# Diagonal blocks of the last 64 queries as full-row products, and an instruction order that counts array-form changes

## The chip, the cores and the metric

The kernel runs on one core of a Trainium2 chip. The metric is the device time of one launch in microseconds. Three runs of the kernel before took 1037.78, 1039.32 and 1043.57 us; their median, 1039.32 us, is the time before. One further execution was profiled.

A core has a matrix engine (TensorE, in the profile PE, with its weight loads shown apart as PEld), a vector engine (VectorE, DVE), a scalar engine (ScalarE, ACT), a general engine (GpSimd, POOL) and a sequencer that issues the DMAs (SyncE, SP). They run their own instruction queues side by side and wait for one another through semaphores.

## The reference

Attention with a decay and a causal mask, then a feed-forward block. The shapes are 8 batches, 8 heads, 576 positions, head size 64, and 4608 tokens by 512, with 2048 hidden columns.

```
scores = q @ k.T / sqrt(64) + cum[:, None] - cum[None, :]    # cum: running sum of log f
scores = where(causal, -1e9, scores);  attn = softmax(scores);  x = attn @ v
h = x @ w_in;  g = h * tanh(log1p(exp(min(h, 20))))          # for h <= 20;  out = g @ w_out
```

576 queries are four blocks of 128 and a last block of 64. This last block of 64 queries, with its own 64 keys, is the "diagonal block" of the title.

## The kernel before

Heads are taken in pairs: one group `g` is two heads (`j` = 0, 1) of one batch, 32 groups in all. Matrices are kept as pairs of 16-bit halves, high and low, so that one exact product is three 16-bit products. Groups 0 to 6 go the old way (`max_items`, `st_items`, `pv_items`): scores are computed transposed (keys in the partitions), the row maxima are found beforehand and put in as an extra row, and P times V takes the exponentials as 32-bit weights. Groups 7 to 31 go the new way (`new_st_items`, `new_pv_items`): scores have queries in the partitions, DVE adds the mask and finds the maxima in one instruction (`highest`), ACT exponentiates, ACT and DVE split the result into halves (`turn`), and a transposing DMA turns it. Behind each batch's attention come the feed-forward products, spread between the later groups' attention.

The last 64 queries of both heads share the 128 partitions: head 0 in 0 to 63, head 1 in 64 to 127. PE works on them with weights of 64 columns, two products side by side in the two halves of the array (`beside`, line 1050). For the diagonal block the weights also have 64 rows only, because keys of head 0 and of head 1 lie in different partitions. Thus PE uses three forms of its array, which the profile writes as rows*columns: 128*128, 128*64 (70 rows count as 128) and 64*64. The places with 64*64 are:

- `tail` (line 1347), new way: the 64 queries of both heads against four key blocks from tile `W` (24 products of form 128*64, in pairs), and then against the diagonal block from tile `V` (6 products of form 64*64, in pairs). `V` is made in `w_` (line 1301): `pv` holds the diagonal scores of both heads in 64 columns, ACT writes their exponentials into `ev`, and these 64 columns are read twice (`two`, line 1318) to fill the 128 columns of `hv`, which a DMA turns into `tv`.
- `blocks` of `pv_items` (line 1399), old way: for `kt == 4` one 32-bit product of 64 rows from tile `T4`, once for each of two heads.
- `two_pass` (line 1161) in `k4`, old way: for groups below 6 the causal mask is added by a product `msk` times `idm` cut to 64 by 64, between products of form 128*64.

The order of instructions on each engine is not the order of the code. `Program` records all operations and runs a list scheduler over them (`forward`, line 410; `backward`, line 370): each engine has a heap of ready operations by rank, and a table of costs says how long each would take. The recorded operations are emitted from one line, so nearly all instructions of the profile carry L317. In that table a PE operation costs its columns divided by the clock; a narrow product beside another one costs 22 ns, and a pair of `beside` adds 53 columns for its second product (line 199). A change of the array's form costs nothing in it. `warmed` (line 319) fills PE's idle time at the start with products of an identity (`idm,idh`).

Of the kernel before, what the change touches and what calls it, by code (L numbers as in the profile page):

```python
# [131 lines left out]
PRIO = 200  # L132
WARM0 = 8000.0
# [21 lines left out]
class Program:  # L155
# [9 lines left out]
    def __init__(self, nc):  # L165
        self.nc = nc
        self.ops = []
        self.banks = []
        self.sets = []
        self.rank = None  # L170
# [10 lines left out]
    def choose(self, *ways):  # L181

        r, w, opts = [], [], []
        for way in ways:
            total, port = 0.0, False
            for eng, method, a, kw in way:
                aps = [(k, x) for k, x in list(enumerate(a)) + list(kw.items()) if hasattr(x, "tensor")]
                w += [z for k, x in aps if k in ("out", "accum_out", 0) for z in self.region(x)]
                r += [z for k, x in aps if k not in ("out", "accum_out", 0) for z in self.region(x)]
                if eng == "scalar":  # L190
                    (r if method == "activation" else w).append(("table", 0, 1, 0, 1))
                if eng == "tensor":

                    w.append((w[0][0] + "/pe", 0, 1, 0, 1))
                port |= self.shared(eng, method, aps)
                cost = self.cost(eng, method, kw, aps)
                if isinstance(cost, tuple) and total:

                    total = (total[0] + 53, total[1] + cost[1], 0)
                else:  # L200
                    total = cost if isinstance(cost, tuple) else total + cost + (80 if total else 0)
            opts.append((eng, way, total, port))
# [8 lines left out]
        self.leads.append(self.lead)  # L211
        func = ways[0][0][3].get("func") if ways[0][0][0] == "scalar" and len(ways) == 1 else None
        self.sets.append("mish" if func == AF.Mish else "exp" if func == AF.Exp else None)
        if self.sets[-1] and self.phase is not None:
# [6 lines left out]
            if hasattr(x, "tensor") and x.space == PSUM})  # L221

# [187 lines left out]
    def forward(self, deps, succ, rank):  # L410
# [13 lines left out]
        table = "exp"  # L424

# [27 lines left out]
        while len(order) < n:  # L453
# [20 lines left out]
            while ripe[q]:  # L474
# [53 lines left out]
            else:  # L528
                if q == "tensor":
# [6 lines left out]
                    half = h  # L536
                elif lock:
# [74 lines left out]
def attn_moe(ctx: ExitStack, tc: tile.TileContext, qk, v, f, w_in, w_out, out):  # L612
# [44 lines left out]
    nc.vector.tensor_scalar(out=mskb2, in0=msk2, scalar1=2.0**100, scalar2=None, op0=ALU.mult)  # L657
    ones = cp.tile([P, P], F32, name="ones")
# [497 lines left out]
    def st_items(g):  # L1156
# [25 lines left out]
        def finish(ps, tag, n, sel):  # L1182
            t4 = n < CH
            e = sp.tile([P, n], F32, name=f"e{tag}{g}", tag="e4" if t4 else "pt", bufs=2 if t4 else NPT)
# [28 lines left out]
        def k4():  # L1213
# [4 lines left out]
            def sel(e):  # L1218
                for j in range(2):
                    tri(e[j * D : (j + 1) * D], 1, D)  # L1220

            finish(ps, "T4", D, sel)
# [10 lines left out]
    def new_st_items(g):  # L1233
# [12 lines left out]
        def highest(o, c, m, first=3e38):  # L1246

            nc.vector.tensor_tensor_reduce(
                out=o, in0=o, in1=m, scale=-0.125, scalar=first, op0=ALU.add, op1=ALU.min,
# [51 lines left out]
        def w_():  # L1301
# [16 lines left out]
            two = ev.unsqueeze(1).to_broadcast([P, 2, D])  # L1318
            hh, ll = (h[:, i].rearrange("p (a d) -> p a d", a=2) for i in range(2))
            nc.choose(*(scaled(hh, two, None, x) for x in HW))  # L1320
            nc.choose(*(sub(ll, two, hh, x) for x in LW_))
# [8 lines left out]
    def new_pv_items(g):  # L1330
# [3 lines left out]
        def products(o, t, k, c, vh, vl, first, last, r=slice(0, P)):  # L1334
            n = 2 if s["V"] is t else 8
            hh, ll = t[r, k, c], t[r, n // 2 + k, c]
# [10 lines left out]
        def tail(o):  # L1347
            for kt in range(5):
                both = []
                for j in range(2):  # L1350
                    r = slice(j * D, (j + 1) * D)
                    if kt < 4:
                        both.append(products(
                            o[r], s["W"], kt, r, s["vh"][:, 2 * kt + j], s["vl"][:, 2 * kt + j], kt == 0, False))
                    else:
                        both.append(products(o[r], s["V"], 0, r, s["vh"][r, 8], s["vl"][r, 8], False, True, r))
                for x in zip(*both):
                    beside(*x)
# [23 lines left out]
    def pv_items(g):  # L1382
# [3 lines left out]
        def pblk(j, kt, qt):  # L1386
            if qt == 4:
                if kt == 4:
                    return "T4", slice(0, D)
# [9 lines left out]
        def blocks(o, j, qt):  # L1399
# [3 lines left out]
            for kt in kts:  # L1403
                tg, c = pblk(j, kt, qt)
                if kt == 4:
                    r = slice(j * D, (j + 1) * D)
                    mm(o[0:m], s[tg][r, c], s["vf"][r, 8], False, False)
# [503 lines left out]
```

## Time and profile before

| | |
|---|---|
| runs, median | 1039.32 us (1037.78 to 1043.57) |
| the profiled execution | 1038.15 us, of which the span of instructions is 1036.4 us |
| mean granted clock of PE | 0.995 |
| PE busy | 1000.0 us, 7779 matmuls |
| DVE busy, ACT busy | 738.9 us, 703.0 us |
| POOL busy | 12.8 us |

Matmuls are pipelined: a row shows a matmul from its start until its result is out, so the next one starts long before. What a matmul occupies of PE is the distance from its start to the next start. Rows that follow each other with the same tiles and engine are merged into one with a count; the first form stands for all of them.

### The profile page before, as it was taken

What the parts mean: (1) busy time and instruction counts of PE and PEld (TensorE: products, weight loads), DVE (VectorE), ACT (ScalarE), POOL (GpSimd) and SP (SyncE); (2) the same over time, 40 slices, a digit from 0 to 9 for tenths busy, and PEclk for the clock granted to TensorE, in tenths of its full rate; (3) what the DMA queues carried; (4) which work ended last, traced back from release to release, by engine and by line L of the source; (5) the groups of instructions that cost most, each with busy time, mean ns of one, the idle gap of its engine ahead of it and who ended that gap; (6) DMA issues with size and microseconds to landing.
All of it is one profiled execution on the core that took longest, in us unless ns stands there. A gap on an engine that the chain in (4) does not pass through costs nothing.

```text
span 1036.4 us, 20830 instructions
## 1 busy us (share of the span) xinstructions
PE 1000.0 (96%) x7779; PEld 561.9 (54%) x7779; DVE 738.9 (71%) x2043; ACT 703.0 (68%) x1309; POOL 12.8 (1%) x73
## 2 busy tenths in 40 slices
PE   5899999999999999999999999999999999999998
PEld 4787565544454455445555455454544555656664
DVE  8878978998776677777766777676766559962432
ACT  7566788978776767777777777787687675433322
POOL 1000001000000000000000000000000000000000
PEclk8999999999999999999999999999999999999999
DMA  7868736599866767677767766767566423001001
GB/s 219 263 185 230 241 105 172 131 216 240 174 138 149 166 138 148 139 177 145 156 136 164 150 153 140 166 141 142 116 123 135 85 56 93 2 3 41 1 1 42
DMA packets 245410, 140.45 MB, mean 136 GB/s; under 512 B 213436, under 2 KB 214012, under 8 KB 245308
## 3 DMA queue, kind: packets, MB, share of 16 engines
q1 hardware_dynamic: 245308, 139.12, 57.8%
q8 instruction: 61, 1.00, 0.4%
q14 instruction: 41, 0.34, 0.1%
HBM read 47.78 MB, written 11.76 MB: 57 GB/s over the span
## 4 chain that ended last, share of the span: by engine, by line
PE 61%; DVE 15%; ACT 10%; DMA 8%; issue 4%; SPq 2%; POOL 0%; DVEq 0%; ACTq 0%; POOLq 0%
PE b L317 61%; DMA pt<-hb 2%; DMA st<-hl 2%; DMA qk<-in_qk_dram 2%; DVE b L317 2%; DVE wall L317 2%; ACT junk L317 2%; SPq L317 2%; ACT hb L317 2%; ACT st L317 1%; DVE hl L317 1%; DVE hb L317 1%; ACT more_e L317 1%; DVE vv L317 1%; DVE x L317 1%
## 5 line engine op out<-in xcount | busy, mean ns | idle before, releaser
L317 PEld LDWEIGHTS <-wall 128*128 128x128 f16 x3372 | 321.6, 98 | 354.4 <-issue 21.2
L317 PE MATMUL b<-gh,wall 128*128 128x512 f16 x1152 | 369.3, 379 | 1.2 <-DVE wall L317 0.7
L317 PE MATMUL b<-xa,wall 128*128 128x512 f16 (+1 forms) x1602 | 344.2, 365 | 6.1 <-ACT me L317 4.1
L317 PE MATMUL b<-gl,wall 128*128 128x512 f16 x576 | 218.2, 379 | 0.0
L317 PE MATMUL b<-st 70*128 70x256 f16 (+10 forms) x978 | 145.6, 280 | 16.9 <-DMA st<-cumd 7.3
L317 DVE SCALAR_TENSOR_TENSOR gl<-me,gsc,gh 128x512 f16<-128x512 f32 x144 | 106.5, 750 | 36.1 <-ACT gh L317 34.6
L317 PEld LDWEIGHTS <-st 128*128 128x128 f16 (+3 forms) x1170 | 91.2, 101 | 72.0 <-issue 26.0
L317 ACT ACTIVATE me<-b,cinv 128x512 f32<-128x512 f32 (+1 forms) x130 | 85.3, 661 | 59.3 <-PE b L317 58.5
L317 PE MATMUL b<-vv,pt 128*128 128x64 f16 (+3 forms) x2492 | 116.4, 207 | 2.8 <-ACT pt L317 1.3
L317 ACT ACT_TABLE_LOAD x74 | 94.9, 1283 | 1.5 <-DVE cinv L317 0.2
L317 DVE CUSTOM_DVE_ANT_0 b<-b,mskw 128x512 f32<-128x512 f32 (+2 forms) x150 | 84.9, 567 | 12.8 <-PE b L317 10.7
L317 ACT ACTIVATE more_e<-b,mn 128x512 f32<-128x512 f32 (+3 forms) x114 | 59.1, 540 | 34.0 <-DVE mn L317 31.8
L317 ACT ACTIVATE st<-b,mn 128x512 f32<-128x512 f32 (+3 forms) x111 | 57.5, 547 | 29.3 <-DVE mn L317 26.6
L317 PEld LDWEIGHTS <-pt 128*128 128x128 f16 (+1 forms) x2100 | 65.0, 101 | 17.4 <-DMA pt<-hb 2.1
L317 DVE TENSOR_TENSOR hb<-st,hb 128x512 f16<-128x512 f32 x75 | 51.6, 689 | 30.9 <-ACT hb L317 28.7
L317 DVE TENSOR_TENSOR hb<-more_e,hb 128x512 f16<-128x512 f32 x75 | 51.4, 688 | 28.5 <-ACT hb L317 28.4
L317 ACT ACTIVATE gh<-me,gsc 128x512 f16<-128x512 f32 x84 | 60.1, 719 | 2.0
L317 DVE TENSOR_SCALAR gh<-me,gsc 128x512 f16<-128x512 f32 x60 | 28.9, 485 | 39.2 <-ACT me L317 38.2
L317 ACT ACTIVATE hb<-st 128x512 f16<-128x512 f32 x75 | 46.8, 627 | 10.0 <-DMA pt<-hb 8.1
L317 ACT ACTIVATE junk<-qk 128x576 bf16<-128x576 f32 x60 | 40.7, 678 | 17.9 <-DMA qk<-in_qk_dram 17.4
L317 ACT ACTIVATE hb<-more_e 128x512 f16<-128x512 f32 x75 | 46.7, 626 | 6.6 <-DMA pt<-hb 6.1
L317 DVE SCALAR_TENSOR_TENSOR hl<-qk,qt,hl 128x576 f16<-128x576 f32 x58 | 46.0, 814 | 5.2 <-DMA st<-hl 3.7
(167 smaller groups left out, 1004.7 us busy)
## 6 DMA issues: line engine op xcount, KB each, us to landing
st<-hl SPq DMA_DIRECT2D x180, 144.0 KB
qk<-in_qk_dram SPq DMA_DIRECT2D x30, 576.0 KB
v<-in_v_dram SPq DMA_DIRECT2D x32, 288.0 KB
out_dram<-ot SPq DMA_DIRECT2D x36, 256.0 KB
wall<-in_w_in_dram SPq DMA_DIRECT2D x16, 512.0 KB
wall<-in_w_out_dram SPq DMA_DIRECT2D x16, 512.0 KB
pt<-hb SPq DMA_TRANSPOSE x150
part<-ot SPq DMA_DIRECT2D x8, 256.0 KB
```

The costliest lines, as they stand in the source:

```text
L317: r = getattr(real[eng], method)(*a, **kw)
```

## The change

Four edits on the diagonal blocks, one on the scheduler.

1. `tail`: the tile `V` becomes block-diagonal over 128 columns, so its three products take all 128 rows and 128 columns and serve both heads at once. They stand at the head of the accumulation, not at its end.
2. `w_`: `highest` for `pv` reads the 64 columns twice, adds a mask of 128 columns that shuts out the other head (`mskv`), and writes 128 columns beside the scores in the same bank; the exponential then covers 128 columns and goes to a fixed tile `evs`, one of two by the group's number.
3. `k4` and `blocks`, old way: the exponentials of both heads go to two diagonal places of `evs`, which is zero elsewhere, with one ACT instruction for each head. The product of `T4` takes 128 rows, with form 128*64.
4. `two_pass`: the mask product takes all 128 rows of `msk` and `idm`, which for 64 columns is form 128*64.
5. `Program`: each PE operation records its form. In `forward` a change of form costs 97 ns at full clock; while PE is in a narrow form, it takes ready operations of the same form first, up to 3000 units of rank ahead of others. The second product of a pair adds 8 columns in place of 53.

```
-                    total = (total[0] + 53, total[1] + cost[1], 0)
+                    total = (total[0] + 8, total[1] + cost[1], 0)
...
+        self.forms.append(self.form(*ways[0][0]) if ways[0][0][0] == "tensor" else None)
...
+    def form(eng, method, a, kw):
+        rows = int(kw["in_"].shape[0] if method == "transpose" else kw["lhsT"].shape[0])
+        cols = int(kw["out"].shape[0])
+        return rows > 64 or (rows + 31) // 32, cols > 64 or (cols + 31) // 32
...
-                if q == "scalar" and f not in (None, table):
+                if q == "scalar" and f not in (None, table) or q == "tensor" and self.forms[x[1]] != form:
...
-                if far is not None and x[0] > far[0] + TSWAP:
+                if far is not None and x[0] > far[0] + (TSWAP if q == "scalar" else 0 if form == (True, True) else MSWAP):
...
+                    if self.forms[i] != form:
+                        form = self.forms[i]
+                        cost += MSW * slow
...
+    evs = cp.tile([P, 2, P], F32, name="evs")
+    nc.gpsimd.memset(evs, 0.0)
+    mskv = cp.tile([P, 2, D], BF16, name="mskv")
+    nc.gpsimd.memset(mskv, -60000.0 * 2.0**100)
+    for j in range(2):
+        r = slice(j * D, (j + 1) * D)
+        nc.gpsimd.tensor_copy(out=mskv[r, j], in_=mskb2[r])
...
-                mm(o[:, 0:tri], msk[0:tri, 0:tri], idm[0:tri, 0:tri], False, False)
+                mm(o[:, 0:tri], msk[:, 0:tri], idm[:, 0:tri], False, False)
...
+            s["T4"] = evs[:, g % 2].rearrange("p (j d) -> p j d", j=2)
+            for j in range(2):
+                r = slice(j * D, (j + 1) * D)
+                e = s["T4"][r, j]
+                nc.scalar.activation(out=e, in_=ps[r, 0:D], func=AF.Exp, scale=0.125)
...
-            highest(pv[:, 0:D], 9, mskb2)
+            two = pv[:, P : 2 * P].rearrange("p (j n) -> p j n", j=2)
+            highest(two, 9, mskv, 3e38, pv[:, 0:D].unsqueeze(1).to_broadcast([P, 2, D]))
...
-            ev = sp.tile([P, D], F32, name=f"ev{g}", tag="e4")
-            exp(ev, pv[:, 0:D], 8)
+            ev = evs[:, g % 2]
+            exp(ev, pv[:, P : 2 * P], 8)
...
         def tail(o):
...
+            for a in products(o, s["V"], 0, slice(0, P), s["vh"][:, 8], s["vl"][:, 8], True, False):
+                mm(*a)
+            for kt in range(4):
+                for x in zip(*(products(
+                        o[r], s["W"], kt, r, s["vh"][:, 2 * kt + j], s["vl"][:, 2 * kt + j], False, kt == 3)
+                        for j, r in enumerate((slice(0, D), slice(D, P))))):
                     beside(*x)
...
-                    r = slice(j * D, (j + 1) * D)
-                    mm(o[0:m], s[tg][r, c], s["vf"][r, 8], False, False)
+                    mm(o[0:m], s[tg][:, j], s["vf"][:, 8], False, False)
```

How the order moves on PE, at the first tail of a new group. Before, the pairs from `W` (tile `pt`) end, six narrow products from `V` (tile `tv`) follow, and then a feed-forward product (`gh`, `wall`). The size at a row's end is that of the output.

```order
L317 LDWEIGHTS pt_138
L317 MATMUL b_0_128<-vv_142,pt_138 64x65
L317 LDWEIGHTS pt_138
L317 MATMUL b_0_128<-vv_142,pt_138 64x65
L317 LDWEIGHTS tv_196
L317 MATMUL b_0_128<-vv_142,tv_196 64x65
L317 LDWEIGHTS tv_196
L317 MATMUL b_0_128<-vv_142,tv_196 64x65
L317 LDWEIGHTS tv_196
L317 MATMUL b_0_128<-vv_142,tv_196 64x64
```

After the change, at the same tail, a full product of the block before (`pt_141`), the three from `V`, and then the first pair from `W`:

```order
L327 LDWEIGHTS pt_141
L327 MATMUL b_0_130<-vv_143,pt_141 128x65
L327 LDWEIGHTS tv_196
L327 MATMUL b_0_130<-vv_143,tv_196 128x65
L327 LDWEIGHTS tv_196
L327 MATMUL b_0_130<-vv_143,tv_196 128x64
L327 LDWEIGHTS tv_196
L327 MATMUL b_0_130<-vv_143,tv_196 128x65
L327 LDWEIGHTS pt_139
L327 MATMUL b_0_130<-vv_143,pt_139 64x65
L327 LDWEIGHTS pt_139
L327 MATMUL b_0_130<-vv_143,pt_139 64x65
```

The products from `V` are three of 128 outputs in place of six of 64, and they stand among full products.

The second place on PE is the end of a later tail (tile `pt_142`). After the change the scores of the last 64 queries of another group (`st`) stand directly behind it, before the feed-forward product that follows:

```order
L327 LDWEIGHTS pt_142
L327 MATMUL b_0_130<-vv_132,pt_142 64x65
L327 LDWEIGHTS st_1_85
L327 MATMUL b_0_123<-st_1_85 64x64
L327 LDWEIGHTS st_1_85
L327 MATMUL b_0_123<-st_1_85 64x64
L327 LDWEIGHTS st_1_88
L327 MATMUL b_0_123<-st_1_88 64x64
```

Before the change the six products from `V` end every such run of narrow products, as in the first fence, and the scores of the last 64 queries stand in runs of their own. Now 14 of the 25 tails have such scores in the same run.

The third place is ACT near the start, at the first exponential of a diagonal block of the old way. Before:

```order
L317 ACTIVATE pt_134<-b_0_119 128x512
L317 ACTIVATE junk_110,wsq<-wall 128x512
L317 ACTIVATE e_0_132<-b_0_122 128x64
L317 ACTIVATE pt_137<-b_0_123 128x512
L317 ACTIVATE pt_138<-b_0_128 128x512
```

After:

```order
L327 ACTIVATE mr_131<-b_0_123 128x128
L327 ACTIVATE junk_112,wsq<-wall 128x512
L327 ACTIVATE evs<-b_0_124 64x64 x2
L327 ACTIVATE pt_134<-b_0_129 128x512
L327 ACTIVATE pt_135<-b_0_121 128x512
```

One instruction of 128 partitions has become two of 64, and it stands before the wide exponentials of this group and not between them.

Over the whole program PE's order holds 249 changes of the array's form before and 169 after, and 141 and 135 filling products.

## Rows read from the trace of the kernel before

**Rows 1.** The page: span, and busy time, share and instructions by engine.
```profile
span 1036.4 us, 20830 instructions
...
PE 1000.0 (96%) x7779; PEld 561.9 (54%) x7779; DVE 738.9 (71%) x2043; ACT 703.0 (68%) x1309; POOL 12.8 (1%) x73
```

**Rows 2.** Stages: length, busy us of PE, PEld, DVE, ACT, POOL; clock, DMA.
```profile
0.00:40.00 40.00, 24.97 (x268) 20.73 (x268) 35.02 (x90) 26.31 (x56) 3.88 (x32) 0.87 0.81 258
40.00:140.00 100.00, 96.12 (x879) 70.81 (x879) 79.99 (x236) 68.33 (x142) 0.81 (x6) 1.00 0.67 198
140.00:300.00 160.00, 156.41 (x1113) 83.77 (x1112) 135.22 (x402) 134.04 (x242) 5.37 (x15) 1.00 0.76 180
300.00:860.00 560.00, 550.57 (x4390) 279.92 (x4389) 389.64 (x1106) 408.82 (x755) 2.77 (x20) 1.00 0.66 138
860.00:1036.40 176.40, 171.96 (x1137) 106.65 (x1135) 99.08 (x214) 65.47 (x116) 0.00 (x0) 1.00 0.08 24
```

**Rows 3.** Waits of PE: for whom, us in total, times, longest.
```profile
PE b L317 <- ACT me L317: 4.1, 7, 1.1
PE b L317 <- ACT st L317: 2.6, 7, 0.8
```

**Rows 4.** Timeline of PE around narrow scores: start, us, instruction, count.
```profile
250.94 0.59 PE L317 MATMUL b<-gh,wall 128*128 128x512 f16 x2
251.37 0.38 PE L317 MATMUL b<-gl,wall 128*128 128x512 f16 x1
251.59 0.38 PE L317 MATMUL b<-gh,wall 128*128 128x512 f16 x1
251.90 0.69 PE L317 MATMUL b<-st 70*64 70x64 f16 x8
```

**Rows 5.** Timeline of PE around an old group's mask products.
```profile
42.10 0.22 PE L317 MATMUL b<-st 128*128 128x128 f16 x1
42.15 0.22 PE L317 MATMUL b<-msk,idm 128*128 128x128 f16 x1
42.30 0.22 PE L317 MATMUL b<-st 128*64 128x64 f16 x1
42.45 0.21 PE L317 MATMUL b<-idm,msk 64*64 64x64 f16 x1
42.59 0.22 PE L317 MATMUL b<-mr,more_e 128*64 128x64 f16 x1
```

**Rows 6.** Timeline of PE: full products from `pt`; the six of a tail's `tv`.
```profile
205.53 1.07 PE L317 MATMUL b<-vv,pt 128*128 128x65 f16 x30
206.44 0.38 PE L317 MATMUL b<-gh,wall 128*128 128x512 f16 x1
...
246.80 0.28 PE L317 MATMUL b<-vv,tv 64*64 64x65 f16 x6
247.02 0.39 PE L317 MATMUL b<-gh,wall 128*128 128x512 f16 x1
```

**Rows 7.** Groups of PE and PEld: count, busy us, mean ns, idle before.
```profile
L317 PE MATMUL b<-vv,tv 64*64 64x65 f16 x100 | 7.0, 202 | 0.0
L317 PE MATMUL b<-vv,e 64*64 64x65 f32 x28 | 4.6, 243 | 0.0
L317 PE MATMUL b<-idm,msk 64*64 64x64 f16 x12 | 2.6, 213 | 0.0
L317 PEld LDWEIGHTS <-pt 128*128 128x128 f16 (+1 forms) x2100 | 65.0, 101 | 17.4 <-DMA pt<-hb 2.1 <-issue 1.7
```

**Rows 8.** Groups of DVE and ACT: the instructions of 64 and 128 columns.
```profile
L317 DVE CUSTOM_DVE_ANT_0 b<-b,mskb 128x128 f32<-128x128 f32 x50 | 15.0, 300 | 4.8 <-PE b L317 3.4
L317 DVE CUSTOM_DVE_ANT_0 b<-b,mskb 128x64 f32<-128x64 f32 x25 | 5.8, 233 | 2.2 <-PE b L317 2.2
L317 ACT ACTIVATE st<-b,mn 128x128 f32<-128x128 f32 x24 | 8.8, 368 | 1.7 <-DVE mn L317 1.7
L317 ACT ACTIVATE e<-b,mn 128x64 f32<-128x64 f32 x25 | 7.8, 313 | 0.6 <-DVE mn L317 0.6
L317 ACT ACTIVATE e<-b 128x64 f32<-128x64 f32 x7 | 1.6, 222 | 3.3 <-PE b L317 3.1
```

More of the change, by code (lines that the diff above doesn't have):

```diff
@@ L132 @@
 PRIO = 200
+MSW = 97.0
+MSWAP = 3000
 WARM0 = 8000.0
@@ L169, in __init__ @@
         self.sets = []
+        self.forms = []
         self.rank = None
@@ L221, in choose @@
             if hasattr(x, "tensor") and x.space == PSUM})
+    @staticmethod
+    def form(eng, method, a, kw):
+        rows = int(kw["in_"].shape[0] if method == "transpose" else kw["lhsT"].shape[0])
+        cols = int(kw["out"].shape[0])
+        return rows > 64 or (rows + 31) // 32, cols > 64 or (cols + 31) // 32
     @staticmethod
@@ L424, in forward @@
         table = "exp"
+        form = (True, True)
         left, half = {}, 0
@@ L1182, in finish @@
         def finish(ps, tag, n, sel):
-            t4 = n < CH
-            e = sp.tile([P, n], F32, name=f"e{tag}{g}", tag="e4" if t4 else "pt", bufs=2 if t4 else NPT)
+            e = sp.tile([P, n], F32, name=f"e{tag}{g}", tag="pt", bufs=NPT)
             nc.scalar.activation(out=e, in_=ps[:, 0:n], func=AF.Exp, scale=0.125)
@@ L1216, in k4 @@
                 two_pass(ps[j * D : (j + 1) * D, 0:D], j, slice(CH, S), slice(CH, S), D)
[L1218 to L1222, printed above, removed]
+            s["T4"] = evs[:, g % 2].rearrange("p (j d) -> p j d", j=2)
[3 more added lines that the diff above has]
+                nc.scalar.activation(out=e, in_=ps[r, 0:D], func=AF.Exp, scale=0.125)
+                if g >= GS:
+                    tri(e, 1, D)
         return [
@@ L1244, in scores, with highest @@
             mm(o, q2[:, j, q0 : q0 + m], k2[:, j, k0 : k0 + n], False, True)
-        def highest(o, c, m, first=3e38):
+        def highest(o, c, m, first=3e38, in_=None):
             nc.vector.tensor_tensor_reduce(
-                out=o, in0=o, in1=m, scale=-0.125, scalar=first, op0=ALU.add, op1=ALU.min,
+                out=o, in0=o if in_ is None else in_, in1=m, scale=-0.125, scalar=first, op0=ALU.add, op1=ALU.min,
                 accum_out=s["mx"][:, c : c + 1])
@@ L1317, in w_ @@
             t = sp.tile([P, 2, P], F16, name=f"tv{g}", tag="tv", bufs=2)
[L1318 to L1321, printed above, removed]
+            nc.choose(*(scaled(h[:, 0], ev, None, x) for x in HW))
+            nc.choose(*(sub(h[:, 1], ev, h[:, 0], x) for x in LW_))
             nc.sync.dma_start_transpose(out=t, in_=h)
@@ L1332, in new_pv_items, with products @@
         s = st[g]
-        def products(o, t, k, c, vh, vl, first, last, r=slice(0, P)):
+        def products(o, t, k, c, vh, vl, first, last):
             n = 2 if s["V"] is t else 8
-            hh, ll = t[r, k, c], t[r, n // 2 + k, c]
+            hh, ll = t[:, k, c], t[:, n // 2 + k, c]
             return [(o, hh, vh, first, False), (o[:, 0:D], hh, vl, False, False), (o, ll, vh, False, last)]
@@ L1347, in tail @@
         def tail(o):
-            for kt in range(5):
-                both = []
-                for j in range(2):
-                    r = slice(j * D, (j + 1) * D)
[L1352 to L1357, printed above, removed]
+            for a in products(o, s["V"], 0, slice(0, P), s["vh"][:, 8], s["vl"][:, 8], True, False):
[4 more added lines that the diff above has]
+                        for j, r in enumerate((slice(0, D), slice(D, P))))):
                     beside(*x)
@@ L1388, in pblk @@
                 if kt == 4:
-                    return "T4", slice(0, D)
+                    return "T4", None
                 return f"T2{j}", slice(256 + D * kt, 320 + D * kt)
@@ L1405, in blocks @@
                 if kt == 4:
-                    r = slice(j * D, (j + 1) * D)
-                    mm(o[0:m], s[tg][r, c], s["vf"][r, 8], False, False)
+                    mm(o[0:m], s[tg][:, j], s["vf"][:, 8], False, False)
                     continue
```

## The prediction

> **What bounds the kernel now.** I read the page's busy shares first. PE is busy for 1000.0 of 1036.4 us, DVE for 738.9, ACT for 703.0 [rows 1]. The stages come next, for the share over the span hides where PE stands idle. In the first 40 us PE is idle for 15.0 us (40.00 − 24.97): that is the start, with loads and preparation ahead of the first scores. From 40 to 860 us it is idle for 3.9 + 3.6 + 9.4 = 16.9 us in 820, and behind 860 for 4.4 us [rows 2]. So from 40 us on PE sets the pace. DVE and ACT come closest from 140 to 300 us, with 135.2 and 134.0 us of 160, 84%. The waits that PE does have are short and scattered: the largest kind from the middle part is seven waits for ACT's `me` with 4.1 us together, none over 1.1 us [rows 3].
>
> A busy PE is not a PE at its peak, so the third view is the distance between starts. A 512-column product is followed by its like after 0.22 us (251.37 to 251.59). When the next product has the form 70*64, it starts 0.31 us later (251.59 to 251.90), and PE was not waiting for data, since the row shows no idle time [rows 4]. At an old group the same is seen three times in a row: 0.05 us from a 128-column product to the next of its form, 0.15 us to the first of form 128*64, 0.15 us from there into 64*64 and 0.14 us out of it [rows 5]. A 64-column product takes about half of the 0.05 us by itself (30 full products of 65 columns took 0.91 us, 0.030 each [rows 6]). So a change of form costs 0.31 − 0.22 = 0.09, 0.15 − 0.05 = 0.10, and 0.15 − 0.03 = 0.12 or 0.14 − 0.03 = 0.11 us. I take 0.095 us: the two readings that compare the same product before and after a change. The bounds are 0.09 and 0.11. This cost stands within PE's busy time and in no wait.
>
> **The change part by part.** Changes of form: PE's order holds 249 before and 169 after, 80 fewer. They come from four places. (a) Each of 25 tails went 128*128, 128*64, 64*64 and back, and now goes 128*128, 128*64 and back: 25 fewer. The count of tails is that of the `tv` products of 65 columns, 100 with four to a tail [rows 7]. (b) The 32-bit products from `T4` are 28 records, two to a product, hence 14 products in 14 accumulations [rows 7]; each dropped one change: 14. (c) Twelve mask products of 64*64 stood between narrow ones [rows 7]; a run of that kind costs two changes where 128*64 lies on both sides, as in rows 5, else one: 21 by the order. (d) The remaining 80 − 60 = 20 are ten runs of narrow products that have been joined to others. At 0.095 us this is 80 × 0.095 = **7.6 us** less on PE (7.2 to 8.8 by the bounds). Laid against the trace, 15 of the 249 lie in the first 40 us, 3 behind 860 us and all others where PE sets the pace.
>
> Products of `V`: six narrow ones with the change behind them took 0.22 us (246.80 to 247.02), so 0.125 without the change; three full ones take 3 × 0.030 = 0.09 [rows 6]. That is 0.035 × 25 = **0.9 us** less. The bounds: each new product might need its weight load in full, 101 ns [rows 7], which would make it 25 × (0.303 − 0.125) = 4.5 us more; and at best the three are free, 3.1 us less. I take the value by the 30 products, because each of those has its own weight load too and still starts 0.030 us after the last.
>
> At this place the Trainium skill speaks against the change. Its page "TensorE: Matmul & The Clock Gate", section "Back-to-back issue gap", says that in a stream of weight load and matmul pairs both set the pace, and that 128-column products come about 81 ns apart. With that, an estimate, 75 products would take 6.1 us and not 2.3, and the sum would be 3.8 us worse than mine. The trace does not agree: its 30 pairs come 30 ns apart.
>
> The products from `T4` stay two records each and keep their columns, and so do the mask products: their rows double, and rows are not what a product's duration goes by here (`vv,e` with 64 rows has 243 ns [rows 7], and I found none longer for more rows). I cost them at nothing.
>
> DVE and ACT: `highest` on the diagonal block goes from 64 to 128 columns, 300 against 233 ns, 25 × 0.067 = 1.7 us of DVE; its exponential from 313 to about 368 ns, 25 × 0.055 = 1.4 us of ACT; in the old way one exponential of 222 ns becomes two, at most 7 × 0.222 = 1.6 us of ACT [rows 8]. The halving of `ev` and the turning DMA had 128 columns already. Together 4.7 us, hidden where PE never waits for these tiles (idle before the `tv` products: 0.0 us [rows 7]), and up to 4.7 us more if every one were on the path. The products of `V` now come first in the tail. They can't be late on that account: the tail still needs all of `W`, whose turning is issued behind that of `V`. POOL gets two memsets and two small copies at the start, when it has 3.9 us of work in 40 [rows 2].
>
> What is late next: PE now asks for everything 8.5 us earlier by the end of the attention part, and the waits of 16.9 us between 40 and 860 us can grow. The order also is a new one at every engine, so no single wait of before has to stand. I add **1.0 us**; the bounds are all 8.5 us given back, and 5 us gained if the order, which now counts what PE really takes, has fewer waits (nearly a third of 16.9). I stay near zero since PE waits for DVE and ACT only one part in fifty, and they have a sixth of their time free even at the tightest stage.
>
> The sum against the profiled execution: 1038.15 − 7.6 − 0.9 + 1.0 = 1030.65 us. The median of the runs stands 1.17 us above that execution, so I forecast 1030.65 + 1.17 = **1031.8 us**, by itself between 1029 and 1034.
>
> **Rivals.** First, PE is shorter, but the waits come back: half or more of 8.5 us turns into waits for DVE and ACT. For it speaks the stage from 140 to 300 us, in which both are at 84% and the first weights, the last old groups and the new ones meet; against it, that stage holds only 37 of the 249 changes. With 5 us given back the time is 1036.
>
> Second, the order gains as well. It now knows 97 ns for a change, which is what the rows show, so an operation is released nearer to when PE is ready for it. Taking away a third of 16.9 us gives 1031.8 − 1.0 − 5 = 1026 us. Against it: most waits of before are single ones of under 1.1 us with a dozen different releasers [rows 3].
>
> Third, and on the other side: the grouping holds banks. While PE is in the narrow form, it takes narrow products ahead of others. In the new order 12 of 25 groups have the 512-column scores of the last queries apart from their diagonal scores (before: 2). The wide `highest` starts from the maximum of the diagonal scores, so a bank that is written early stays taken until the others have come. If each of these 12 and of the 14 tails that are joined with scores made PE wait 0.6 us (the mean of seven waits for `me`, 4.1 / 7 [rows 3]), it would cost 26 × 0.6 = 15.6 us and give 1030.8 + 15.6 = 1046. It decides from 0.53 us per place, where the 8.5 saved and 5.2 more are used up. Against it: where they are apart, it is mostly by one tail's length, some 30 products and under 1 us, and there are four score banks.
>
> Fourth, the change does what it says, but full products need their weight load on the path: a full product from `V` then costs 0.101 us, the 4.5 us of above in place of the 0.9 saved, which gives 1031.8 + 5.4 = 1037 us. It is the skill's rule carried to its end; the 30 products in 0.91 us speak against it.
>
> **How the numbers follow.** A measurement of this kernel can tell 0.5% from no change, 5.2 us: faster is below 1034.1, slower above 1044.5. The forecast has a chance of 0.57, all of it on the faster side; the gaining order 0.15, faster; the waits that come back 0.19, no change; the weight loads 0.03, no change; the held banks 0.06, slower. Hence faster 0.72, same 0.22, slower 0.06. The range from 1026 to 1038 us holds the forecast, nearly all of the two cases of no change, and about half of the gaining order.
>
> **What would show it.** In the profile after, PE has no 64*64 form; the `tv` products are 75 of form 128*128, three in about 0.09 us; a feed-forward product still starts 0.31 us ahead of a narrow one; PE's busy time falls by 7 to 9 us to about 992, and its idle time from 40 to 860 us stays between 12 and 22 us. I am wrong in the size if the busy time does not fall by that much, in the hiding if the idle time grows by more than 5 us, and about the start if the first 40 us become longer, which I cost at nothing since the order of PE there is nearly the same.

## The result, and the profile after

The changed kernel takes 1029.12 us (median of 4 runs, 1027.53 to 1030.69), beside 1040.03 us of the kernel before in the same comparison (4 runs): the ratio is 0.9893 [0.9871, 0.9915]. A second comparison gave 1030.03 beside 1039.8 us, 0.9914 [0.9895, 0.9934]. So 9.8 to 10.9 us went, where 7.5 were forecast (1039.32 − 1031.8). The profiled execution is the fastest of the first four, 1027.53 us.

The page's span, and its line of busy time by engine:

```profile
span 1025.7 us, 20649 instructions
...
PE 988.8 (96%) x7698; PEld 556.1 (54%) x7698; DVE 737.0 (72%) x2040; ACT 707.0 (69%) x1315; POOL 13.4 (1%) x77
```

Beside [rows 1], PE is busy for 11.2 us less, and the span is 10.7 us shorter. Span less busy time, which is PE's idle time over the whole run, is 36.9 us after and was 36.4. So nearly all that was gained stands within PE's busy time, as the change of form did, and PE waits about as much as it did. A part of such a difference is the clock: the profile grants PE either the full clock (1.00) or half of it (0.50), and PE was busy at half clock for 6.8 us in the profile before and for 4.3 us here. About half of that time, 3.4 and 2.2 us, is lost (an estimate).

The stages, with the columns of [rows 2] (length; busy us of PE, PEld, DVE, ACT, POOL; clock, DMA share, GB/s):

```profile
0.00:40.00 40.00, 24.05 (x267) 19.79 (x267) 34.69 (x91) 26.23 (x57) 4.83 (x35) 0.91 0.80 249
40.00:140.00 100.00, 94.71 (x903) 71.06 (x903) 86.29 (x256) 75.31 (x159) 0.77 (x7) 1.00 0.75 209
140.00:300.00 160.00, 156.26 (x1148) 83.57 (x1149) 129.13 (x385) 130.57 (x238) 5.14 (x16) 1.00 0.75 175
300.00:860.00 560.00, 551.90 (x4351) 280.31 (x4349) 400.40 (x1131) 412.67 (x754) 2.64 (x19) 1.00 0.67 140
860.00:1025.70 165.70, 161.85 (x1039) 101.40 (x1037) 86.46 (x182) 62.23 (x110) 0.00 (x0) 1.00 0.06 20
```

From 40 to 860 us PE is idle for 5.3 + 3.7 + 8.1 = 17.1 us; it was 16.9 [rows 2]. The first 40 us hold as many products as before (267 and 268), so the start did not become longer. What is gained shows as a shorter last stage, 165.7 us and 1039 products in place of 176.4 us and 1137: the work behind 860 us is what had not been reached by then.

PE's waits (whom for, us in total, times, longest), with the two kinds of [rows 3]:

```profile
PE b L327 <- ACT me L327: 6.7, 9, 1.7
...
PE b L327 <- ACT st L327: 3.4, 5, 1.4
...
PE b L327 <- ACT evs L327: 0.4, 1, 0.4
```

The waits for `me` and `st` rose by 2.6 and 0.8 us, the others fell by 2.3 us together; all of PE's waits went from 31.4 to 32.5 us. On `evs`, the new tile, PE waited once, for 0.4 us.

The timeline of PE: an old group's mask products (as in [rows 5]), a tail (as in [rows 6]), and narrow scores behind a feed-forward product (as in [rows 4]); start, us, instruction, count:

```profile
43.61 1.90 PE L327 MATMUL b<-vv,pt 128*128 128x65 f32 x16
45.44 0.46 PE L327 MATMUL b<-st 128*64 128x512 f16 x4
45.70 0.23 PE L327 MATMUL b<-idm,msk 128*64 128x64 f16 x2
45.73 0.23 PE L327 MATMUL b<-mr,more_e 128*64 128x64 f16 x2
45.77 0.23 PE L327 MATMUL b<-st 128*64 128x64 f16 x2
45.92 1.26 PE L327 MATMUL b<-vv,pt 128*128 128x65 f32 x10
...
241.66 1.08 PE L327 MATMUL b<-vv,pt 128*128 128x65 f16 x30
242.58 0.25 PE L327 MATMUL b<-vv,tv 128*128 128x65 f16 x3
242.76 0.57 PE L327 MATMUL b<-vv,pt 128*64 128x65 f16 x24
243.26 0.39 PE L327 MATMUL b<-gh,wall 128*128 128x512 f16 x1
...
247.84 0.38 PE L327 MATMUL b<-gh,wall 128*128 128x512 f16 x1
248.15 0.69 PE L327 MATMUL b<-st 70*64 70x64 f16 x8
```

The mask products (45.70) now start 0.03 us ahead of their neighbours of the same form, with nothing between, where [rows 5] had 0.14 to 0.15 on either side. The three products from `tv` take 0.18 us up to the first narrow product (242.58 to 242.76), and 0.097 of it is the change of form that stood there before too: 0.08 for three. And a feed-forward product still starts 0.31 us ahead of a narrow one (247.84 to 248.15): the price of a change is what it was, there are fewer.

The price can be summed over a whole trace, from the distance between starts less what the same product takes among its like (stretches at half clock and places with a wait left out). Before, 239 changes take 23.5 us, 0.098 each; after, 163 take 15.7 us, 0.096 each. That is 7.8 us less. Too short a wait leaves no idle time in these rows, since a product's row (0.38 us) is longer than the distance to the next (0.31 us). That these distances are the price and no waits for data is shown by their evenness: the 14 from a feed-forward product to a 70*64 one are all between 0.307 and 0.310 us.

One place gained more than a change. The last narrow 32-bit product from `pt`, the product of `T4` (tiles `e` and `evs`, two records) and the next full product, before and after:

```profile
68.35 0.22 PE L317 MATMUL b<-vv,pt 128*64 128x65 f32 x1
68.50 0.33 PE L317 MATMUL b<-vv,e 64*64 64x65 f32 x2
68.75 0.32 PE L317 MATMUL b<-vv,pt 128*128 128x65 f32 x1
...
68.79 0.22 PE L327 MATMUL b<-vv,pt 128*64 128x65 f32 x1
68.85 0.28 PE L327 MATMUL b<-vv,evs 128*64 128x65 f32 x2
69.06 0.32 PE L327 MATMUL b<-vv,pt 128*128 128x65 f32 x1
```

From the first row to the third it is 0.40 us before and 0.27 after; over the 14 places the medians are 0.406 and 0.267. So 0.139 us went at each, and not only the 0.095 of one change: beside the change ahead of it, the first record of the product became 0.048 us shorter. That is 0.6 us more than the prediction has.

Groups of PE, DVE and ACT that answer to [rows 7, 8] (count, busy us, mean ns, idle before):

```profile
L327 PE MATMUL b<-vv,tv 128*128 128x65 f16 x50 | 6.3, 192 | 0.0
...
L327 PE MATMUL b<-vv,tv 128*128 128x64 f16 x25 | 4.8, 193 | 0.0
L327 PE MATMUL b<-vv,evs 128*64 128x65 f32 x28 | 3.9, 222 | 0.0
...
L327 PE MATMUL b<-idm,msk 128*64 128x64 f16 x12 | 1.7, 200 | 0.0
...
L327 DVE CUSTOM_DVE_ANT_0 b<-b,mskv 128x128 f32<-128x128 f32 x25 | 7.6, 303 | 2.7 <-PE b L327 2.7
...
L327 ACT ACTIVATE evs<-b,mn 128x128 f32<-128x128 f32 x25 | 9.1, 363 | 4.3 <-DVE mn L327 4.3
...
L327 ACT ACTIVATE evs<-b 64x64 f32<-64x64 f32 x14 | 3.0, 215 | 0.5 <-PE b L327 0.2
```

No group has the form 64*64 any more. `highest` on the diagonal costs 1.8 us more (7.6 against 5.8), the exponentials 2.7 us more (9.1 + 3.0 against 7.8 + 1.6), nearly as worked out ahead (1.7 and 3.0).

### The profile page after: what moved, and what is told of

The parts are those of the page before. It is cut to its first block, busy times and chain, and to the rows that moved or that the text cites. A ratio compares the mean times of both kernels' runs of the same rounds, so it can differ in the third digit from the quotient of the medians.

```text
span 1025.7 us, 20649 instructions
## 1 busy us (share of the span) xinstructions
PE 988.8 (96%) x7698; PEld 556.1 (54%) x7698; DVE 737.0 (72%) x2040; ACT 707.0 (69%) x1315; POOL 13.4 (1%) x77
## 4 chain that ended last, share of the span: by engine, by line
PE 60%; ACT 6%; DVE 5%; DMA 4%; issue 2%; SPq 0%; ACTq 0%; DVEq 0%
PE b L327 60%; DMA pt<-hb 3%; DVE b L327 2%; ACT hb L327 1%; ACT L327 1%; DVE vv L327 1%; ACT more_e L327 1%; ACT st L327 1%; DMA st<-hl 1%; ACT me L327 1%; DVE x L327 1%; DVE xp L327 1%; DVE hb L327 1%; ACT ot L327 0%; DMA v<-in_v_dram 0%
## 5 line engine op out<-in xcount | busy, mean ns | idle before, releaser
L327 PE MATMUL b<-st 70*128 70x128 f16 (+12 forms) x978 | 144.9, 280 | 15.9 <-DMA st<-cumd 6.8
L327 DVE CUSTOM_DVE_ANT_0 b<-b,mskw 128x256 f32<-128x256 f32 (+2 forms) x150 | 84.5, 566 | 8.4 <-PE b L327 6.3
L327 ACT ACTIVATE gh<-me,gsc 128x512 f16<-128x512 f32 x89 | 63.5, 719 | 2.1
L327 DVE TENSOR_SCALAR gh<-me,gsc 128x512 f16<-128x512 f32 x55 | 26.6, 484 | 37.8 <-ACT me L327 36.8
L327 PEld LDWEIGHTS b<-vv,pt 128*128 128x128 f32 x392 | 45.2, 183 | 5.6 <-ACT pt L327 2.5
```

The lines of the kernel that those rows point to most:

```text
L327: r = getattr(real[eng], method)(*a, **kw)
```

## The experiments

All times are medians of several runs, beside runs of the kernel before on the same chip; those of one set share them (before: 1039.8 in the first, 1039.48 in the second, 1040.13 us in the third). The kernel after ran in the first set only; the three figures of before lie within 0.7 us, and a difference of 1 us between sets decides nothing. "Changes" counts the changes of form in PE's order. The last three columns are of the profiled execution: PE's busy time, the part of it in stretches with a granted clock of 0.50, and idle, which is span less busy time.

| kernel | changes | us | ratio | PE busy | at half clock | PE idle |
|---|---|---|---|---|---|---|
| before | 249 | 1039.8 | 1 | 1000.0 | 6.8 | 36.4 |
| after (repeated) | 169 | 1030.03 | 0.9914 [0.9895, 0.9934] | 991.7 | 15.8 | 35.8 |
| blocks alone | 195 | 1036.26 | 0.9972 [0.9957, 0.9986] | 997.1 | 16.0 | 36.6 |
| scheduler alone | 231 | 1034.95 | 0.9961 [0.9946, 0.9976] | 1000.7 | 16.0 | 33.8 |
| `V` in three places | 312 | 1050.98 | 1.0105 [1.0083, 1.0128] | 1010.0 | 13.1 | 39.2 |
| extra DVE and ACT work | 168 | 1030.76 | 0.991 [0.9898, 0.9923] | 991.7 | 9.8 | 37.9 |
| no grouping | 191 | 1034.13 | 0.9949 [0.993, 0.9968] | 995.5 | 13.2 | 38.8 |
| pair at 53 columns | 162 | 1033.86 | 0.995 [0.9932, 0.9968] | 990.2 | 8.6 | 41.0 |
| scores as one | 156 | 1021.88 | 0.983 [0.9814, 0.9846] | 989.9 | 11.0 | 33.2 |
| other ranks 1 | 162 | 1035.2 | 0.9961 [0.9942, 0.998] | 988.9 | 4.4 | 42.2 |
| other ranks 2 | 168 | 1031.1 | 0.992 [0.9891, 0.9949] | 994.6 | 14.6 | 38.3 |
| ranks 2, scores as one | 156 | 1027.36 | 0.9894 [0.9865, 0.9923] | 992.1 | 11.7 | 36.0 |
| no grouping, scores as one | 184 | 1034.17 | 0.9944 [0.9922, 0.9966] | 995.6 | 13.1 | 37.9 |

The columns of the profile are read together. If half of the time at half clock is taken off the busy time (an estimate), it goes with the count of changes: 1003.5 us at 312, 996.6 at 249, 992.6 at 231, 989 from 195 to 184, and 984 to 987 from 169 to 156. The idle time, from 33 to 42 us, does not go with that count.

**The changed kernel again.** The same file, to have its size with a second set of runs.

> The changed kernel again, as the yardstick of this set. Its order holds 169 changes of the array's form, that of before 249. Theory A (each change that goes saves about 0.097 us of PE, and nothing else of size happens): the first timing was 1029.1 against 1040.0, 10.9 us, of which A explains 80 x 0.097 + 0.9 = 8.7; a repeat should come out at 8 to 11 us below before. Theory B (the new order brings a good part by fewer waits): the same here, the kernels below tell the two apart.

It gave 1030.03 us (4 runs, 1029.55 to 1030.93): 9.8 us less than before.

**The block edits alone.** The blocks as after, the scheduler as before (no price, no grouping, 53 columns):

```
-                    total = (total[0] + 8, total[1] + cost[1], 0)
+                    total = (total[0] + 53, total[1] + cost[1], 0)
...
-        self.forms.append(self.form(*ways[0][0]) if ways[0][0][0] == "tensor" else None)
+        self.forms.append((True, True) if ways[0][0][0] == "tensor" else None)
```

> The four edits on the diagonal blocks alone; the scheduler prices as before (no form, 53 for the second of a pair). Its order holds 195 changes, 54 fewer than before. Theory A: 54 x 0.097 + 0.9 for the products of V = 6.1 us less than before, about 1034 where before has 1040. Theory B: less than half of the changed kernel's gain, so 1035 to 1040, as its order is not the new one.

1036.26 us, 3.5 less than before. With 54 changes fewer the count alone gives 54 × 0.097 = 5.2 and the products of `V` 0.9, hence 1034. That is missed by 2.6 us. The order holds 162 filling products, 21 more than before; at 0.055 us each they can be some 1.2 us of this, an estimate. The rest is not explained.

**The scheduler edits alone**, on the blocks of before (edit 5 of the change and nothing else):

```
-                    total = (total[0] + 53, total[1] + cost[1], 0)
+                    total = (total[0] + 8, total[1] + cost[1], 0)
...
+                    if self.forms[i] != form:
+                        form = self.forms[i]
+                        cost += MSW * slow
```

> The kernel before with the scheduler's edit alone (price of a form change, grouping, 8 for the second of a pair); the diagonal blocks stay narrow. Its order holds 231 changes, 18 fewer than before. Theory A: 18 x 0.097 = 1.7 us less than before, about 1038. Theory B: 4 to 6 us less, 1034 to 1036.

1034.95 us, 4.9 less, where 18 changes fewer are worth 1.7. In its profile PE's busy time is that of before, and its idle time is 2.6 us shorter. But this execution has one of the stretches at half clock of the last section, from 38.1 to 48.4 us, with PE busy throughout: 16.0 us of busy time at half clock, where before has 6.8. That hides some 4.6 us of shorter busy time (half of the difference, an estimate), and the idle time that is less lies in that stretch and behind it, 3.4 us from 40 to 300 us in place of 7.5. So that this order gains by its waits is not shown; 3.2 of the 4.9 us stay without a cause. Parts and whole do not add up either: 3.5 + 4.9 = 8.4 of 9.8 us.

**The three products of `V` apart.** In the tail, one of them stands behind each of the first three key blocks, so that each needs a change of form before and behind it:

```
             for kt in range(4):
...
                     beside(*x)
+                if kt < 3:
+                    mm(*vs[kt])
```

> The changed kernel with the three full products of V put one each behind the first three key blocks of the tail, so that PE goes from narrow to full and back three times in each of 25 tails. Same products, same sizes; its order holds 312 changes, 143 more than the changed kernel. Theory A: 143 x 0.097 = 13.9 us more than the changed kernel, about 1043. If the price seen between starts were covered in the end by other waits, it would stay within 5 us of the changed kernel.

1050.98 us, 21.0 more than after. The order holds 143 changes more: 143 × 0.097 = 13.9 us by the price. The timeline of PE in one tail:

```profile
247.88 0.20 PE L327 MATMUL b<-vv,tv 128*128 128x64 f16 x1
248.02 0.28 PE L327 MATMUL b<-vv,pt 128*64 128x65 f16 x6
248.23 0.20 PE L327 MATMUL b<-vv,tv 128*128 128x65 f16 x1
248.37 0.29 PE L327 MATMUL b<-vv,pt 128*64 128x65 f16 x6
248.59 0.39 PE L327 MATMUL b<-gh,wall 128*128 128x512 f16 x1
```

One full product that takes 0.03 us among its like holds PE for 0.14 us when a narrow one follows (247.88 to 248.02, and 248.23 to 248.37). A wait for data would not be so regular: behind the 50 products of 65 columns the distance is 0.133 to 0.135 us, 0.104 above the product's own, a little more than at the other kinds of change. Summed from the starts as above, 303 changes take 30.0 us here, and 161 take 15.5 us in the repeated kernel after. The page gives 18.3 us more of busy time than in the repeated kernel after, and 3.4 more idle. The changes cover 14.5 of the 18.3, and 15 more filling products (150 against 135) of 0.055 us another 0.8; the rest, some 3, I could not assign.

**Extra work on DVE and ACT.** `highest` and the exponential of the diagonal block are each issued twice, 25 times:

```
+            highest(two, 9, mskv, 3e38, pv[:, 0:D].unsqueeze(1).to_broadcast([P, 2, D]))
             highest(ps, 8, mskw[:, 0:1].to_broadcast([P, CH]), s["mx"][:, 9:10])
...
             exp(ev, pv[:, P : 2 * P], 8)
+            exp(ev, pv[:, P : 2 * P], 8)
```

> The changed kernel with the DVE instruction on the diagonal scores (0.300 us) and its exponential on ACT (0.37 us) issued twice in each of the 25 new groups, with the same result: 7.5 us more of DVE and 9.2 us more of ACT, against the 1.7 and 1.4 us that the change added there. Its order holds 168 changes. If this work is hidden, as the prediction has it: within 2 us of the changed kernel, 1029 to 1032. If it stands on the path that sets the end: 8 to 17 us more, 1038 to 1047.

1030.76 us, against 1030.03 and 1029.12 of the kernel after. The groups, with the two instructions (count, busy us, mean ns):

```profile
L327 DVE CUSTOM_DVE_ANT_0 b<-b,mskv 128x128 f32<-128x128 f32 x50 | 15.1, 302 | 2.9 <-PE b L327 2.5
...
L327 ACT ACTIVATE evs<-b,mn 128x128 f32<-128x128 f32 x50 | 18.4, 368 | 4.7 <-DVE mn L327 4.3
```

7.5 us more on DVE and 9.3 us more on ACT, one behind the other in each of 25 groups, cost about 1 us, no more than the runs scatter. The order is a new one here too, which by itself can move the time by several us (below), so this shows that most of the added work is hidden, and not what each us of it costs. The 4.5 us that the change itself adds there are a quarter of it.

**Without grouping, and with the old price of a pair.** Two single edits of the scheduler, each on the kernel after:

```
-MSWAP = 3000
+MSWAP = 0
```

> The changed kernel with the grouping off (no rank ahead for operations of the narrow form), the price of a change still counted. Its order holds 191 changes, 22 more than the changed kernel. Theory A: 2.1 us more than the changed kernel, 1032. If the grouping is what holds waits down (theory B): 1034 to 1036. If the grouping holds banks and costs waits: as the changed kernel or less, 1027 to 1030.

```
-                    total = (total[0] + 8, total[1] + cost[1], 0)
+                    total = (total[0] + 53, total[1] + cost[1], 0)
```

> The changed kernel with 53 columns for the second product of a pair in the scheduler's costs, as before the change, and not 8. Its order holds 162 changes, 7 fewer. Theory A: 0.7 us less than the changed kernel, about 1029. If the truer cost of pairs is what brought fewer waits (theory B): 1032 to 1035.

1034.13 and 1033.86 us, 4 us more than after each. Without grouping there are 22 changes more, worth 2.1 us. With 53 columns there are 7 fewer, and the time is still longer: PE's busy time is short (990.2), and its idle time is 41.0 us, 4 to 5 more than in the two profiles of after. So the count of changes is not all that an order is worth. In these two orders 2 and 7 of 25 groups have their 512-column scores more than eight products away from the diagonal ones, against 10 in the kernel after by the same count: standing apart does not make a kernel slow.

**The eight score products of the last 64 queries as one operation.** The planner can no longer put anything between them:

```
-            for o, k in ((pv[:, 0:D], slice(CH, S)), (ps, slice(0, CH))):
-                beside(*((
-                    o[j * D : (j + 1) * D], q1[0 : KM - 1, j, CH:S], k1[0 : KM - 1, j, k], True, False)
-                    for j in range(2)))
-                beside(*((
-                    o[j * D : (j + 1) * D], q2[:, j, CH:S], k2[:, j, k], False, True) for j in range(2)))
+            beside(*(
+                (o[j * D : (j + 1) * D], *x)
+                for o, k in ((pv[:, 0:D], slice(CH, S)), (ps, slice(0, CH)))
+                for y in (0, 1) for j in range(2)
+                for x in (((q1[0 : KM - 1, j, CH:S], k1[0 : KM - 1, j, k], True, False),
+                           (q2[:, j, CH:S], k2[:, j, k], False, True))[y],)))
```

> The changed kernel with the eight score products of the last 64 queries (diagonal and wide) recorded as one operation, so that no other product can come between them. Its order holds 156 changes of form, 13 fewer than the changed kernel (169). Theory A (only changes count, 0.097 us each): 1.3 us less than the changed kernel, about 1028.5 where it has 1030. Theory B' (any new order has other waits, by some 3 us either way): 1026 to 1032.

1021.88 us (4 runs, 1021.06 to 1024.81): 8.2 less than the repeated kernel after, and the fastest version here. The profiled execution is the slowest of the four. Its page, and its waits for `me`:

```profile
span 1023.1 us, 20621 instructions
...
PE 989.9 (97%) x7690; PEld 556.9 (54%) x7690; DVE 737.2 (72%) x2045; ACT 704.8 (69%) x1314; POOL 14.3 (1%) x77
```

```profile
PE b L327 <- ACT me L327: 2.8, 4, 1.3
```

13 changes fewer are 1.3 us. The idle time is 2.7 us shorter than in the repeated kernel after (33.2 against 35.8), and the wait for `me`, 6.7 and 7.4 us in the two profiles of after, is down to 2.8. That makes 4.0 us, and the two profiled executions differ by 4.7 (1029.55 and 1024.81). This is no full account: the execution also has less time at half clock (11.0 against 15.8 us), and `me` alone does not make a kernel fast, since with the extra work on DVE and ACT that wait is 3.9 us, at 1030.76. The other 3.5 us of the 8.2 lie between this execution and the other runs of the kernel, which left no trace.

**The same rules with other ranks.** The planner adds a small random number to each operation's rank, so that the same edits come out as another order. Two seeds, and the second again with the scores as one operation:

```
-SEED = 122
-NZ = 0
+SEED = 1
+NZ = 30
```

> The changed kernel with a random number of up to 30 added to each operation's first rank, so that the same rules over the same products give another order. 162 changes of form (169), the diagonal and the wide scores of the last queries apart in 14 of 25 groups (10). Theory A (the count of changes alone): 0.7 us less than the changed kernel, 1029. Theory C (each order has waits of its own, some 3 to 5 us either way, beside the count): anywhere from 1024 to 1036, and another figure than the next kernel. Theory D (the scores that stand apart cost waits): 1 to 3 us more than the changed kernel.

> As the kernel before it, with another draw of the random numbers. 168 changes of form, scores apart in 17 of 25 groups. Theory A: 1030. Theory C: from 1024 to 1036, not the same as the first draw. Theory D: 2 to 5 us more than the changed kernel, the slowest of the two draws.

> The second draw with the eight score products of the last queries as one operation, so apart in none of 25 groups. 156 changes of form. Theory A: 1.2 us less than the second draw. Theory C: from 1022 to 1033. Theory D (standing together saves waits): 5 us or more less than the second draw, as it was 8 us less than the changed kernel without the draw, 1021.9 against 1030.

1035.2 us with seed 1 (12 runs, 1031.64 to 1038.27), 1031.1 with seed 2 (the same lines, `SEED = 2`; 6 runs, 1030.18 to 1034.66), with 162 and 168 changes. The page of seed 1:

```profile
span 1031.1 us, 20650 instructions
...
PE 988.9 (96%) x7708; PEld 555.5 (54%) x7708; DVE 730.3 (71%) x2033; ACT 713.8 (69%) x1326; POOL 14.6 (1%) x77
```

PE's busy time is that of the kernel after, and its idle time is 42.2 us in place of 36.9. So of two orders made by the same rules, with nearly the same count, one lies 5 us above the one that the change came with, and the other no further from it than the runs scatter. The 5 us are not the clock: over the 12 runs the mean granted clock has a median of 0.9915, as over the four runs of the repeated kernel after. With seed 2 the scores as one operation gave 1027.36, 3.7 us less; the intervals of these two overlap.

**The scores as one, without grouping.** `MSWAP = 0` and the edit of the scores together.

> The changed kernel with the grouping off (1034.1, scores apart in 2 of 25 groups, 191 changes) and the eight score products of the last queries as one operation: apart in none, 184 changes. Theory A: 0.7 us less than with the grouping off alone, 1033.4. Theory D: nothing more than that, since they stood together before. Theory C: 1029 to 1037. If recording them as one operation helps in itself, by the scheduler's view of them: 1028 or less.

1034.17 us, beside 1034.13 with `MSWAP = 0` alone: nothing gained. So the 8 us of this edit are not the price of the scores themselves. It is worth 8.2, 3.7 and 0 us in three orders.

## Why the prediction was right, and where it was not

**Price and number of changes: right.** 80 fewer at 0.097 us are 7.8 us (7.6 forecast), and the sums over the two traces differ by the same 7.8 us. The price shows at a feed-forward product ahead of a narrow one (0.31 − 0.22) and, with 0.104 us, in the tails of the experiment with three places, where 143 changes more made the kernel 21.0 us slower. The prediction took the missing idle time in a row as proof that PE waits for no data; a wait that short shows in no row, and the proof is the evenness of the distances.

**Products of `V`: right.** Three of them take 0.08 us (0.18 − 0.097); 0.09 was forecast, and 0.24 is an estimate by the figure of the page of the Trainium skill that the prediction named ("TensorE: Matmul & The Clock Gate", section "Back-to-back issue gap": 81 ns apiece, three times). That figure is for products of 128 columns, and those of `V` have 65 or 64, so the prediction carried it to another size; but the trace does not agree at 128 columns either, with 0.05 us from one such product to the next in [rows 5], each with its own weight load. The rival of weight loads on the path falls with this.

**DVE and ACT hidden: right.** 1.8 and 2.7 us were added, and three to four times as much again moved the time by about 1 us.

**Products of `T4`: undersized.** The prediction costs one change less at each of 14 places, 0.095 us, and the product itself at nothing; 0.139 us went, 0.6 us more in all. That rows don't lengthen a product holds: with 128 rows its records have 222 ns, with 64 they had 243. The remark that none was longer for more rows is wrong as it stands, since the 32-bit products of 128*128 have a mean of 277 ns in the trace before; these have 128 columns of the array too.

**The term that was mis-sized: the waits.** I added 1.0 us, on the ground that PE asks for everything earlier and in a new order. PE's idle time changed by +0.5 us in the first profile and by −0.6 in the repeated one (36.4 before, 36.9 and 35.8 after), so nothing of that size came. The terms as they were measured, 7.8 for changes, 0.8 for `V` and 0.6 for `T4`, make 9.2 of the 9.8 to 10.9 us; the remaining 0.6 to 1.7 us are within what the runs of one program differ by and have no cause shown. The busy time fell by 11.2, where I gave 7 to 9, and in the repeated run by 8.3. The two runs are of one program, so some 3 us of that line belong to the execution and not to the kernel: PE was busy at half clock for 4.3 us in the first and for 15.8 in the second.

The second rival, the gaining order, is neither shown nor excluded: the scheduler edits alone gained 4.9 us, of which changes of form are 1.7, and the profile leaves open what the rest is. There is no sign that a planner with the right price waits less as a rule: with other ranks the same planner gave 42.2 and 38.3 us of idle time, more than before the change. That the waits stayed level is therefore partly luck of the order. With the ranks of seed 1 the same change would have been worth 4.9 us, half as much, and I had no term for this spread except the bounds of the waits (8.5 given back to 5 gained), which held it.

**The slower rival, held banks: not seen.** By the count above (more than eight products between; the prediction's 2 and 12 count shorter distances too), the groups whose scores stand apart rose from 1 to 10, and no wait of 0.6 us each came with them: PE's waits went from 31.4 to 32.5 us in all. With the second seed 17 groups stand apart, at 1031.1 us; without grouping 2, at 1034.1. The number does not go with the time.

**What stays open.** Why keeping the eight score products together gives 8 us in one order and none in another: about half of it lies between two profiled executions, where fewer changes and shorter waits can account for it and the clock differs too, and for the other half there is no trace. What 3.2 of the 4.9 us of the scheduler edits alone are, and why the blocks alone gained 2.6 us less than worked out, is open as well. The block edits were not taken apart further (tail, `T4`, mask products), since single parts of 1 to 2 us would drown in what a new order can do by itself.

## What to carry to other kernels

Where an engine is busy for 96% and its waits are short, look at the distance between the starts of neighbours: a price that stands in no wait (here 0.097 us for each change of the array's form) can be read there and multiplied by a count from the instruction order. Edits that pass through a planner bring a new order, and a new order can be worth several us of its own in either direction: try an edit of that size in two or three orders before its parts are given a value, and let the range have this spread. Before two profiles are compared by an engine's busy time, look at how long each ran at half clock. Work can then be made indivisible where the planner tears it apart; here that was the best of all versions, but it too gained in some orders only.

## What the runs showed of the hardware

The change of form costs nearly the same between all pairs of forms that the order holds (128*128, 128*64, 64*64 before), 0.098 us in the mean over 239 places before and 0.096 over 163 after, with medians of 0.09 to 0.11 for the single kinds, at the granted clock of 1.00. The mask products of 128 rows take no longer than those of 64 (200 ns, 213 in [rows 7]).

Not expected were stretches at half clock long after the start. In the repeated kernel after, and in the kernel with the scheduler edits alone, the stages there (columns as above; the seventh figure behind the length, after POOL, is the granted clock):

```profile
70.00:75.70 5.70, 4.25 (x47) 3.38 (x42) 5.42 (x17) 5.22 (x15) 0.03 (x1) 1.00 0.65 187
75.70:82.50 6.80, 6.80 (x49) 6.22 (x49) 3.73 (x14) 3.23 (x7) 0.11 (x1) 0.50 0.79 197
```

```profile
30.00:38.00 8.00, 5.48 (x73) 4.17 (x71) 7.83 (x19) 4.66 (x12) 0.10 (x1) 1.00 1.02 393
38.00:48.00 10.00, 10.00 (x65) 9.07 (x65) 4.82 (x15) 4.07 (x12) 0.24 (x1) 0.51 0.76 221
```

The clock is at 1.2 GHz for 6.8 and for about 10 us, and PE, which had been idle for 25% and 32% of the stretch ahead, is then busy throughout. In the first profile of the same program PE is idle for the same share of the same stretch, and the clock does not fall:

```profile
70.00:75.70 5.70, 4.25 (x45) 3.53 (x42) 5.39 (x18) 5.29 (x13) 0.00 (x0) 1.00 0.61 151
75.70:82.50 6.80, 5.68 (x67) 4.48 (x66) 5.22 (x15) 4.67 (x10) 0.12 (x1) 1.00 0.80 204
```

So these rows do not tell what decides it. The same 6.80 us hold 67 products at the full clock and 49 at half. The kernel with the scores as one has such a stretch at 251.2 us, for 3.4 us, and the blocks alone at 874.3 us. The timeline of PE in the repeated run:

```profile
80.03 0.31 PE L327 MATMUL b<-st 128*128 128x128 f16 x1
80.13 0.31 PE L327 MATMUL b<-msk,idm 128*128 128x128 f16 x1
80.24 0.31 PE L327 MATMUL b<-st 128*128 128x128 f16 x1
```

Products of 128 columns stand 0.10 to 0.11 us apart, where [rows 5] has 0.05. Over a whole run it shows in the mean granted clock: in the 12 runs with seed 1, the four at 0.990 took 1035.2 to 1038.3 us and the three at 0.995 took 1031.6 to 1034.2. So a few us between runs of one program can come from here, and what one profile shows of PE's busy time is only as good as that. It is not the only source: over the ten runs of the blocks alone clock and time do not go together (1035.37 us at 0.990, 1039.78 at 0.992).
